# Threshold attention and two MoE layers: turned row maxima in `zt`'s spare columns, a start from two queues, decoding jobs further apart

## The chip, the cores and the metric

One core of a Trainium2 chip. The metric is the device time of one execution in microseconds; for the kernel before it is 1000.67 us, the median of 3 runs (996.61 to 1002.05).

## What is computed

Attention over 4 batches of 8 heads, 576 positions, head size 64, with a threshold under each row's maximum; then two feed-forward layers on the 2304 tokens.

```python
scores = scale * np.matmul(q, k.transpose(0, 1, 3, 2))
thresh = np.max(scores, axis=-1, keepdims=True) - tau
scores = np.where(scores >= thresh, scores, -1000000000.0)
attn = np.exp(scores - np.max(scores, axis=-1, keepdims=True))
attn = attn / (np.sum(attn, axis=-1, keepdims=True) + 1e-09)
x = np.matmul(attn, v)                      # then (tokens, heads * 64)
h = x @ w_in                                # 512 -> 2048
g = np.where(h >= 1, h, np.where(h <= -1, 0.0, (h + 1) ** 2 / 4))
y = g @ w_out
h2 = y @ w_in2                              # 512 -> 1024
solu = h2 * softmax(h2)
ln = (solu - mean(solu)) / np.sqrt(var(solu) + 1e-06) * g_ln
out = ln @ w_out2
```

## The kernel before

The program is in three stages: attention, the first feed-forward layer, the second. Matmuls take every operand as a high and a low part, so most products run as several. Only the attention stage and its start are touched by the diff.

Attention goes over 16 pairs of heads. A head's q and k (loaded side by side by `load_kq` into `nat`) are transposed together (`transpose_kq`, tile `tr`), split into a high half `q_st` on ScalarE and a low half `lo` on VectorE (`split_kq`), and copied by DMA into the stacked operands `k_both` (planes `k_st` and `k_on`), `q_st` and `q_m` (`stack_k`, `stack_q`). The scores are computed twice. First by rows: `scores` makes five tiles `sc` a head, `row_max` (VectorE) takes each row's maximum into `mcol`, and `row_shift` (two steps on ScalarE, three on GpSimd) makes of it the shift `mr`, 128 x 10. `shift_turn` transposes `mr` on TensorE (tile `tm`), `shift_store` copies it out on ScalarE (`mt`) and writes it by a DMA on ScalarE's queue into two more rows of `q_m`. Then by columns: `shifted` makes the transposed scores `zt` with the shift already subtracted; `expo` (ScalarE) takes the exponential `e`, `mask` (VectorE) sets to zero what lies under the threshold, `p_split` makes `phi` (ScalarE) and `plo` (GpSimd), and `values` multiplies them with v into `av`, three units later. `store_head` copies the sum out (`xs`).

A pair is 9 units. The order in which a unit's work is issued is a string in the table `ORDER`, a letter for each piece: E is `zt` and `e`, S a score, x a row maximum, M the mask, v and V values, P a transposition or a turn, A ScalarE's work on a shift or on v, T DMAs and other late work, F the split, J a step of a decoding job. The dictionaries `first_`, `late_`, `pe_` and so on hold what each unit does. The attention starts at unit `U0`; pair p's first `zt` is in unit 9p, and its scores run in the units `S_UNITS` before and after it.

`sc`, `zt`, `tr` and `tm` all take a tile of the PSUM pool `ps_r`, of 3 slots of two banks each. In a `zt` tile columns 288 to 511 of each bank are unused. `jobs` decodes and splits eight blocks of weights for the first feed-forward group meanwhile (VectorE, ScalarE and GpSimd), a new block every `JOB_EVERY` units.

## Time and profile before

| | |
|---|---|
| median of 3 runs | 1000.67 us |
| the profiled execution | 997.45 us |
| its span | 995.6 us |
| TensorE busy | 953.3 us (96%) |
| VectorE, ScalarE, GpSimd busy | 707.0, 499.3, 604.0 us |
| attention, 150 to 250 us: TensorE, VectorE, ScalarE, GpSimd busy | 94.70, 79.28, 70.10, 80.95 us |

A span is from the first to the last instruction of an execution; the time also holds what lies around it. The share of TensorE is a mean over stages: near the whole in the feed-forward stages, less in the attention, little in the first 20 us. In rows, PE is TensorE, PEld its weight loads, DVE VectorE, ACT ScalarE, POOL GpSimd, and SPq and ACTq the issuing of DMAs from SP and ScalarE. A row's L number is the line of the kernel.

### The profile page before, as it was taken

What the parts mean: (1) busy time and instruction counts of PE and PEld (TensorE: products, weight loads), DVE (VectorE), ACT (ScalarE), POOL (GpSimd) and SP (SyncE); (2) the same over time, 40 slices, a digit from 0 to 9 for tenths busy, and PEclk for the clock granted to TensorE, in tenths of its full rate; (3) what the DMA queues carried; (4) which work ended last, traced back from release to release, by engine and by line L of the source; (5) the groups of instructions that cost most, each with busy time, mean ns of one, the idle gap of its engine ahead of it and who ended that gap; (6) DMA issues with size and microseconds to landing.
All of it is one profiled execution on the core that took longest, in us unless ns stands there. A gap on an engine that the chain in (4) does not pass through costs nothing.

```text
span 995.6 us, 15113 instructions
## 1 busy us (share of the span) xinstructions
PE 953.3 (96%) x5232; PEld 840.2 (84%) x5232; DVE 707.0 (71%) x1128; ACT 499.3 (50%) x926; POOL 604.0 (61%) x573
## 2 busy tenths in 40 slices
PE   4999999999999999999999999999999999999998
PEld 3889888898898898889988998899889988888886
DVE  3678777778778765598858885887766576566661
ACT  3576776676676667444433333333334434434433
POOL 6477777887897788677535653555357804443422
PEclk9899999999999999999999999999999999999999
DMA  6555566566665421322221222122301214444443
GB/s 157 121 130 135 132 132 164 135 156 145 157 149 113 103 67 33 99 76 66 83 74 58 70 65 74 45 74 72 117 22 54 64 42 118 127 117 126 125 125 92
DMA packets 89885, 99.89 MB, mean 100 GB/s; under 512 B 50032, under 2 KB 62640, under 8 KB 89808
## 3 DMA queue, kind: packets, MB, share of 16 engines
q1 hardware_dynamic: 89424, 98.76, 38.7%
q8 instruction: 41, 0.67, 0.3%
q14 instruction: 36, 0.29, 0.1%
q10 hardware_dynamic: 384, 0.16, 0.1%
HBM read 55.13 MB, written 15.88 MB: 71 GB/s over the span
## 4 chain that ended last, share of the span: by engine, by line
PE 63%; DVE 14%; ACT 6%; POOL 6%; issue 6%; DMA 2%; SPq 2%; ACTq 1%; POOLq 0%; DVEq 0%
PE y L788 19%; PE h L750 19%; PE av L424 7%; PE zt L376 6%; PE sc L303 4%; DVE e L392 3%; POOL plo L401 2%; PE o L943 2%; PE h L832 2%; ACT e L387 2%; DVE so L860 2%; PE tr L260 2%; DVE so L887 2%; DVE st L848 1%; DVE so L872 1%
## 5 line engine op out<-in xcount | busy, mean ns | idle before, releaser
L401 POOL TENSOR_TENSOR plo<-e,phi 128x576 fp32r<-128x576 f32 x144 | 206.2, 1437 | 68.3 <-ACT phi L400 65.6
L771 POOL TENSOR_TENSOR gl<-cl,gh 128x512 fp32r<-128x512 f32 (+1 forms) x80 | 100.4, 1256 | 166.1 <-ACT gh L770 92.7
L788 PE MATMUL y<-gh,wg 128*128 128x512 f32 (+1 forms) x640 | 186.8, 373 | 0.0
L750 PE MATMUL h<-xh,wg 128*128 128x512 f32 (+1 forms) x640 | 184.1, 369 | 0.7 <-DVE e L392 0.7
L392 DVE SCALAR_TENSOR_TENSOR e<-zt,ntau,e 128x576 f32<-128x576 f32 x144 | 116.8, 812 | 78.6 <-ACT e L387 77.8
L387 ACT ACTIVATE e<-zt 128x576 f32<-128x576 f32 x144 | 93.7, 651 | 84.9 <-PE zt L376 69.2
L788 PEld LDWEIGHTS y<-gh,wg 128*128 128x128 f32 x640 | 118.8, 188 | 17.1
L750 PEld LDWEIGHTS h<-xh,wg 128*128 128x128 f32 x640 | 118.5, 188 | 17.4 <-DVE e L392 0.9
L788 PE MATMUL y<-gl,wg 128*128 128x512 f32 (+1 forms) x320 | 120.0, 375 | 0.5 <-POOL gl L771 0.4
L316 DVE TENSOR_REDUCE mcol<-sc 128x1 f32<-128x576 f32 x160 | 116.7, 748 | 3.2 <-PE sc L303 2.8
L750 PE MATMUL h<-xl,wg 128*128 128x512 f32 (+1 forms) x320 | 118.0, 369 | 0.0
L767 ACT ACTIVATE cl<-cl,half 128x512 f32<-128x512 f32 (+1 forms) x80 | 54.4, 680 | 98.3 <-DVE cl L766 98.0
L943 PE MATMUL o<-wg,ln 128*128 128x512 f32 x432 | 103.0, 394 | 0.4 <-ACT ln L906 0.4
L770 ACT CAST gh<-cl 128x512 fp32r<-128x512 f32 (+1 forms) x80 | 46.3, 579 | 111.6 <-DVE cl L769 105.0
L832 PE MATMUL h<-wg,y 128*128 128x512 f32 x432 | 101.1, 390 | 0.0
L943 PEld LDWEIGHTS o<-wg,ln 128*128 128x128 f32 x432 | 80.7, 188 | 19.9 <-ACT ln L906 1.8
L400 ACT CAST phi<-e 128x576 fp32r<-128x576 f32 x144 | 96.2, 668 | 0.9 <-DVE e L392 0.9
L832 PEld LDWEIGHTS h<-wg,y 128*128 128x128 f32 x432 | 81.0, 188 | 16.8
L907 POOL TENSOR_TENSOR ln<-land,ln 128x1024 fp32r<-128x1024 f32 x16 | 38.8, 2427 | 91.7 <-ACT ln L906 91.7
L766 DVE TENSOR_SCALAR cl<-h 128x512 f32<-128x512 f32 (+1 forms) x80 | 50.6, 632 | 56.2 <-PE h L750 52.3
L376 PE MATMUL zt<-q_st,k_both 128*128 128x288 f32 x320 | 75.6, 318 | 7.0 <-ACT mt L343 5.2
L303 PE MATMUL sc<-k_both,q_st 128*128 128x288 f32 x320 | 72.2, 308 | 5.3 <-DMA q_st<-lo 3.5
(107 smaller groups left out, 1871.9 us busy)
## 6 DMA issues: line engine op xcount, KB each, us to landing
raw<-in_moe_w_in_dram SPq DMA_DIRECT2D x24, 512.0 KB
raw<-in_moe_w_out_dram SPq DMA_DIRECT2D x24, 512.0 KB
k_both<-q_st SPq DMA_DIRECT2D x30, 288.0 KB
sq<-so SPq DMA_DIRECT2D x64, 128.0 KB
land<-sq SPq DMA_DIRECT2D x16, 512.0 KB
k_both<-lo SPq DMA_DIRECT2D x32, 144.0 KB
q_st<-lo SPq DMA_DIRECT2D x32, 144.0 KB
x<-xs SPq DMA_DIRECT2D x32, 144.0 KB
```

The source lines that it names most:

```text
L303: nc.tensor.matmul(ps[:, c, 0:HS], lhsT=st[j][i][r, n * P : n * P + P], rhs=kk[j][i][r, o + c * HS : o + (c + 1) * HS], start=(st is q_st) ...
L316: nc.vector.tensor_reduce(mc[:, n : n + 1], sc_ps.pop((h, n))[:, :, 0:HS], axis=AXES.XY, op=ALU.max, negate=True)
L376: nc.tensor.matmul(ps[:, c, 0:HS], lhsT=st, rhs=mv[:, c * HS : (c + 1) * HS], start=(m == 0), stop=(m == len(todo) - 1),)
L387: nc.scalar.activation(out=e, in_=st_ps[u][:, :, 0:HS], func=ACTF.Exp)
L392: nc.vector.scalar_tensor_tensor(out=e, in0=st_ps.pop(u)[:, :, 0:HS], scalar=ntau[:, 0:1], in1=e, op0=ALU.is_ge, op1=ALU.mult)
L400: nc.scalar.copy(hi, e)
L401: (nc.vector if u - NU in LO_DVE or u < NU - UNITS and u % UNITS in LO_UNITS else nc.gpsimd).tensor_tensor(lo, e, f32(hi), op=ALU.subtract)
L750: nc.tensor.matmul(ps, lhsT=a[:, kk, f], rhs=m[:, kk, :], start=(n == 0 and kk == 0), stop=(n == 2 and kk == KD - 1),)
L771: nc.gpsimd.tensor_tensor(gl, cl, f32(gh), op=ALU.subtract)
L788: nc.tensor.matmul(y_ps[c][d], lhsT=a[:, jj, ds_], rhs=m, start=(jj == 0 and n == 0), stop=(jj == JG - 1 and n == 2),)
L832: nc.tensor.matmul(ps[g], lhsT=a[:, kk, :], rhs=wg_t["in2", g][s][:, kk, :], start=(n < 2), stop=(n >= 6 * KD - 2),)
L943: nc.tensor.matmul(ps, lhsT=a[:, f, :], rhs=wg_t["out2", f // 4][m][:, f % 4, :], start=(n == 0), stop=(n == len(terms) - 1))
```

## The change

Three things are changed in the attention stage.

- **The turn.** `shift_turn` writes into columns 288 to 415 of the first bank of a unit's `zt` tile, behind `zt`'s matmuls, and `shift_store` follows that unit's `expo`. Before, it took a slot of its own at the end of a unit (`TURN_AT` 3); now it stands in the unit behind (`TURN_AT` 4): a pair's turns are in its unit 2 and in unit 7 of the pair before. Only the first head, whose turn comes before unit 0, still has a slot of its own.
- **The start.** `U0` is -10 instead of -18. The first pair's loads go alternately to SP's and ScalarE's queue. `split_first` replaces the first pair's `stack_k`: `k_st` and `k_on` are copied straight out of PSUM (ScalarE, VectorE), `q_m` on GpSimd. v of the first pair and half of the third pair's loads are issued from ScalarE. The second pair is transposed between the first pair's scores, its scores start in other units (`S_FIRST`), and `keep_warm` adds 18, 24 and four single transposes whose result nobody reads. The first weight block's load comes behind the stack copies, in unit -4.
- **Decoding.** Blocks start 16, 16, 16, 16, 17, 17, 12 and 10 units apart instead of 14.

```diff
-    U0 = -18
+    U0 = -10
     T_A, T_B = -16, -10
     S_UNITS = (-10, -9, -7, -7, -6, -5, -4, -3, -3, -2)
-    TURN_AT = 3
-    JOB_EVERY = 14
+    S_FIRST = ((-8, -7, -6, -5, -4, -3, -2, -1, -1, 0), (-8, -8, -7, -6, -6, -5, -4, -3, -3, -2))
+    WARM = (18, 24, 1)
+    TURN_AT = 4
+    JOB_EVERY = (16, 16, 16, 16, 17, 17, 12, 10)
...
-    FAST = 2
     V_POOL = 10
     LO_UNITS = ()
     NORM = (13, 6, 4)
     LO_DVE = ()
-    T_FIRST = (-17, -17)
-    T_SECOND = (-13, -2)
+    T_FIRST = (-10, -10)
+    T_SECOND = (-6, -1)
+    SPLIT_SECOND = (-3, 0)
...
+    def load_kq(p, other=nc.sync):
         t = early_p.tile([P, 2, NM + 1, 2, D], F32, tag="nat", name="nat", bufs=2)
         r0 = 2 * p * S
         two = q_rows[r0 : r0 + 2 * S, :].rearrange("(j s) d -> j s d", j=2)
-        for j in range(2):
-            nc.sync.dma_start(
-                t[:, j, 0:NM, 1, :], two[j, 0:M4, :].rearrange("(p t) d -> p t d", t=NM)
-            )
-        nc.sync.dma_start(t[0:64, :, NM, 1, :], two[:, M4:S, :].rearrange("j s d -> s j d"))
         k0 = k_rows[r0 : r0 + M4, :].rearrange("(p t) d -> p t d", t=NM)
         k1 = k_rows[r0 + M4 + P : r0 + 2 * S, :].rearrange("(p t) d -> p t d", t=NM)
+        rest = [
+            (t[0:64, j, NM * (1 - j), 0, :], k_rows[r0 + M4 + 64 * j : r0 + M4 + 64 * j + 64, :]) for j in range(2)
+        ]
+        main = [(t[:, j, 0:NM, 1, :], two[j, 0:M4, :].rearrange("(p t) d -> p t d", t=NM)) for j in range(2)]
+        nc.sync.dma_start(*main[0])
+        other.dma_start(t[0:64, :, NM, 1, :], two[:, M4:S, :].rearrange("j s d -> s j d"))
         nc.sync.dma_start(t[:, 0, 0:NM, 0, :], k0)
+        other.dma_start(*rest[0])
+        nc.sync.dma_start(*main[1])
+        other.dma_start(*rest[1])
         nc.sync.dma_start(t[64:P, 1, 0:NM, 0, :], k1[0:64])
-        nc.sync.dma_start(t[0:64, 1, 1 : NM + 1, 0, :], k1[64:P])
-        for j in range(2):
-            nc.sync.dma_start(t[0:64, j, NM * (1 - j), 0, :], k_rows[r0 + M4 + 64 * j : r0 + M4 + 64 * j + 64, :])
+        other.dma_start(t[0:64, 1, 1 : NM + 1, 0, :], k1[64:P])
...
     def stack_k(h):
         j, i = buf(h)
-        kh = f32(q_st[j][i][0:D, 0:S])
         o = slice(key_off(h), key_off(h) + S)
-        if h < FAST:
-            nc.scalar.copy(k_on[j][i][0:D, o], kh)
-            nc.scalar.copy(q_m[j][i][0:D, 0:S], f32(q_st[j][i][D:P, 0:S]))
-            nc.sync.dma_start(f32(k_st[j][i][0:D, o]), f32(k_on[j][i][0:D, o]))
-        else:
-            nc.sync.dma_start(f32(k_both[j][i][0:D, :, o]), kh.unsqueeze(1).to_broadcast([D, 2, S]))
+        kh = f32(q_st[j][i][0:D, 0:S]).unsqueeze(1).to_broadcast([D, 2, S])
+        nc.sync.dma_start(f32(k_both[j][i][0:D, :, o]), kh)
         nc.sync.dma_start(f32(k_st[j][i][D:P, o]), f32(tr_t[h][0:D, :]))
-        if h < FAST:
-            return
         nc.sync.dma_start(f32(q_m[j][i][0:D, 0:S]), f32(q_st[j][i][D:P, 0:S]))
 
     def stack_q(h):
         j, i = buf(h)
         nc.sync.dma_start(f32(q_st[j][i][0:D, 0:S]), f32(tr_t.pop(h)[D:P, :]))
+
+    def split_first():
+
+        srcs = [tr_t[h] for h in range(2)]
+        for h in range(2):
+            split_kq(h)
+            j, i = buf(h)
+            o = slice(key_off(h), key_off(h) + S)
+            nc.scalar.copy(k_st[j][i][0:D, o], srcs[h][0:D])
+            nc.vector.tensor_copy(k_on[j][i][0:D, o], srcs[h][0:D])
+            nc.sync.dma_start(f32(k_st[j][i][D:P, o]), f32(tr_t[h][0:D, :]))
+            stack_q(h)
+            nc.gpsimd.tensor_copy(q_m[j][i][0:D, 0:S], f32(q_st[j][i][D:P, 0:S]))
+
+    def keep_warm(n):
+
+        ps = ps_av.tile([P, 2, 512], F32, tag="av", name="av")
+        for _ in range(n):
+            nc.tensor.transpose(ps[:, 0, 0:P], ident, ident)
...
-    def shift_turn(h):
-        ps = ps_r.tile([P, 1024], F32, tag="r", name="tm")
-        nc.tensor.transpose(ps[0 : 2 * NTI, 0:P], f32(mr_t.pop(h)).rearrange("p l n -> p (l n)"), ident)
-        mr_t[h] = ps
+    def shift_turn(h, ps=None):
+
+        if ps is None:
+            ps = ps_r.tile([P, 2, 512], F32, tag="r", name="tm")
+        tm = ps[0 : 2 * NTI, 0, HS : HS + P]
+        nc.tensor.transpose(tm, f32(mr_t.pop(h)).rearrange("p l n -> p (l n)"), ident)
+        mr_t[h] = tm
 
     def shift_store(h):
         j, i = buf(h)
         mt = att_p.tile([2 * NTI, P], F32R, tag="mt", name="mt", bufs=2)
-        nc.scalar.copy(mt, mr_t.pop(h)[0 : 2 * NTI, 0:P])
+        nc.scalar.copy(mt, mr_t.pop(h))
         nc.scalar.dma_start(f32(q_m[j][i][R1:R3, :]), f32(mt))
...
+        for h in turn_in.get(u, ()):
+            shift_turn(h, ps)
         st_ps[u] = ps
...
-            self.todo, self.depth = [(t, every, True) for t in todo], depth
+            self.todo, self.depth = [(t, n, True) for t, n in zip(todo, every)], depth
...
+    load_kq(0, nc.scalar)
     nc.scalar.activation(out=warm, in_=one, func=ACTF.Exp)
-    load_kq(0)
...
-            at(first_, t + 1, split_kq, h)
-            at(late_, t + (STACK[0] if h >= FAST else 1), stack_k, h)
-            at(late_, t + (STACK[1] if h >= FAST else 1), stack_q, h)
+            if p:
+                t = t + 1 if p > 1 else SPLIT_SECOND[j]
+                at(first_, t, split_kq, h)
+                at(late_, t + (STACK[0] - 1 if p > 1 else 0), stack_k, h)
+                at(late_, t + (STACK[1] - 1 if p > 1 else 1), stack_q, h)
             at(last_, UNITS * p + (4, 8)[j] + LAGV, store_head, h)
-        if p > 1:
+        if p > 2:
             at(late_, UNITS * p + T_A - 5, load_kq, p)
         if p:
-            at(late_, UNITS * p - 16, load_v, p)
-        at(act_, UNITS * p + V_AT, split_v, p)
+            at(late_, UNITS * p - 16 if p > 1 else -5, load_v, p)
+        if p:
+            at(act_, UNITS * p + V_AT, split_v, p)
+    at(late_, -2, split_v, 0)
...
+        s_units = S_FIRST[p] if p < 2 else S_UNITS
+        for n, d in enumerate(s_units):
             at(s_at, UNITS * p + d, None, 2 * p + n // NTI, n % NTI)
         for j in range(2):
-            t = UNITS * p + S_UNITS[NTI * j + NTI - 1]
+            t = UNITS * p + s_units[NTI * j + NTI - 1]
             at(act_, t + 1, row_shift, 2 * p + j)
-            at(pe_, t + TURN_AT, shift_turn, 2 * p + j)
-            at(act_, t + TURN_AT, shift_store, 2 * p + j)
+            t += TURN_AT if p else 2
+            if t < 0:
+                at(pe_, t, shift_turn, 2 * p + j)
+                at(act_, t, shift_store, 2 * p + j)
+            else:
+                turn_in.setdefault(t, []).append(2 * p + j)
...
                 expo(u)
+                for h in turn_in.get(u, ()):
+                    shift_store(h)
...
-    jobs.step()
     load_kq(1)
-    load_v(0)
-    setup_fill(True)
-    at(late_, T_FIRST[1] + 1, setup_fill, False)
+    setup_fill(0, nc.gpsimd)
+    setup_fill_v()
+    keep_warm(WARM[0])
+    at(pe_, U0 + 1, keep_warm, WARM[1])
+    at(first_, U0 + 1, split_first)
+    at(late_, U0 + 1, load_v, 0, nc.scalar)
+    at(late_, U0 + 1, load_kq, 2, nc.scalar)
+    at(late_, U0 + 1, setup_ones)
+    at(late_, U0 + 1, setup_fill, 1, nc.gpsimd)
+    at(late_, 0, setup_fill, 2, nc.gpsimd)
+    at(late_, -4, jobs.step)
+    for u in (-8, -7, -5, -4):
+        at(late_, u, keep_warm, WARM[2])
```

The rows of the kernels' order show three places. First SP at the start: what is issued up to the first pair's stack copies (128x4x64, 64x2x64 and so on are the loads of q and k; names with 98, 101, 103 and 106 are the first pair's operands). Before, from the second pair's last load:

```order
L227 DMA nat<-in_k_dram 64x64 x2
L237 DMA v_nat_113<-in_v_dram 128x2x256
L243 DMA v_nat_113<-in_v_dram 64x64 x2
L281 DMA k_both_98<-k_both_98 64x576
L284 DMA k_both_98<-lo 64x576
L291 DMA q_st_103<-lo 64x576
```

And of the change:

```order
L231 DMA nat<-in_k_dram 64x64
L232 DMA nat<-in_k_dram 64x4x64
L233 DMA nat<-in_k_dram 64x4x64
L301 DMA k_both_98<-lo 64x576
L290 DMA q_st_103<-lo 64x576
```

No v and no weight block stand ahead of the stack copies now, and the copy of the high half is gone.

Second, TensorE at the first head's turn of a pair, where unit 6 gives way to unit 7. Before:

```order
L424 MATMUL av<-plo,v_hi_116 128x288
L337 MATMUL tm<-ident,mr 10x128 [waits DVE_49,Pool_49]
L376 MATMUL zt<-q_st_107,k_both_102 128x288 [waits Activation_49]
L376 MATMUL zt<-q_st_107,k_both_102 128x288
```

And of the change:

```order
L398 MATMUL zt<-q_st_107,k_both_102 128x288 [waits DVE_49]
L398 MATMUL zt<-q_st_107,k_both_102 128x288
L398 MATMUL zt<-q_m_112,k_both_102 128x288 x2
L358 MATMUL zt<-ident,mr 10x128 [waits Pool_49]
L448 MATMUL av<-phi,v_hi_116 128x288 [waits Activation_49]
```

The turn stands behind `zt` and waits for GpSimd alone; `zt` no longer waits for ScalarE.

Third, ScalarE at the same turn. Before:

```order
L343 CAST mt<-tm 10x128 [waits DMAHW5_49,PE_49]
L344 DMA q_m_111<-mt 2x5x128 [waits DMAHW6_49,Activation_49]
L387 ACTIVATE e<-zt 128x576 [waits PE_49,Pool_49]
L436 COPY xs<-av 128x576 [waits PE_49]
L400 CAST phi<-e 128x576 [waits DVE_49]
```

And of the change:

```order
L411 ACTIVATE e<-zt 128x576 [waits PE_49]
L364 CAST mt<-zt 10x128 [waits DMAHW3_49]
L365 DMA q_m_111<-mt 2x5x128 [waits DMAHW4_49,Activation_49]
L460 COPY xs<-av 128x576 [waits DMAHW5_49,PE_49]
L424 CAST phi<-e 128x576 [waits DVE_49]
```

The exponential moved ahead of the copy and its DMA. On VectorE the mask behind such an exponential has new waits:

```order
L416 SCALAR_TENSOR_TENSOR e<-zt,ntau,e 128x576 [waits Activation_49] x2
L416 SCALAR_TENSOR_TENSOR e<-zt,ntau,e 128x576 [waits PE_49,Activation_49,Pool_49]
L334 TENSOR_REDUCE mcol<-sc 128x1 [waits PE_49] x2
```

Its row names TensorE beside ScalarE, where the masks of the two units before name ScalarE alone.

## Rows read from the trace of the kernel before

**Rows 1.** Busy time of each engine in stretches of the program (us, busy, instruction counts, granted clock, DMA share, GB/s)

```profile
150.00:250.00 100.00, 94.70 (x676) 88.78 (x674) 79.28 (x111) 70.10 (x133) 80.95 (x81) 1.00 0.64 152
...
500.00:600.00 100.00, 100.00 (x480) 87.65 (x480) 77.22 (x116) 35.83 (x59) 51.28 (x40) 1.00 0.21 66
```

**Rows 2.** Waits of TensorE, 60 to 385 us (waiter, waited for: us, times, longest)

```profile
PE tr L260 <- DVE e L392: 7.5, 11, 0.8
PE zt L376 <- ACT mt L343: 4.8, 14, 0.3
...
PE tm L337 <- POOL mr L330: 1.4, 5, 0.4
```

**Rows 3.** The chain in order of time, 150 to 200 us (start, us, what)

```profile
163.56 0.64 PE tr L260 x5
...
168.85 0.11 PE tm L337
168.96 0.55 PE zt L376 x4
...
182.14 0.29 PE tm L337
...
182.76 0.79 PE zt L376 x4
...
194.81 0.86 PE tr L260 x5
```

**Rows 4.** Timeline, unit 2 of a pair (start, us, engine, line, out<-in, idle before)

```profile
191.79 0.43 PE L376 MATMUL zt<-q_m,k_both 67*128 67x288 f32 x2
...
192.25 0.25 ACT L343 CAST mt<-tm 10x128 fp32r<-10x128 f32 x1
...
192.53 0.62 ACTq L344 DMA_DIRECT2D q_m<-mt  x1
...
193.25 0.65 ACT L387 ACTIVATE e<-zt 128x576 f32<-128x576 f32 x1 [0.75 <-PE av L424]
...
193.94 0.82 DVE L392 SCALAR_TENSOR_TENSOR e<-zt,ntau,e 128x576 f32<-128x576 f32 x1 [1.29 <-ACT e L387]
```

**Rows 5.** Timeline, 0 to 24 us: loads, splits, first stack copy, first score

```profile
1.19 1.33 SPq L217 DMA_DIRECT2D nat<-in_q_dram  x2
...
6.38 1.09 PE L260 MATMUL tr<-ident,nat 128*128 128x128 f32 x4 [6.38 <-POOL q_m L188]
...
8.15 0.74 ACT L268 ACTIVATE q_st<-tr,scale 128x576 fp32r<-128x576 f32 x1 [5.93 <-PE tr L260]
...
8.93 0.82 DVE L269 SCALAR_TENSOR_TENSOR lo<-tr,scale,q_st 128x576 fp32r<-128x576 f32 x1 [4.73 <-ACT q_st L268]
...
10.20 0.66 ACT L279 CAST k_both<-q_st 64x576 fp32r<-64x576 f32 x1
...
13.02 1.11 SPq L243 DMA_DIRECT2D v_nat<-in_v_dram  x2
...
14.26 0.52 SPq L281 DMA_DIRECT2D k_both<-k_both  x1
...
18.24 0.82 PE L303 MATMUL sc<-k_both,q_st 128*128 128x288 f32 x2 [3.46 <-DMA q_st<-lo]
```

**Rows 6.** The chain in order of time, 0 to 90 us

```profile
15.46 2.64 DMA q_st<-lo
```

**Rows 7.** Timeline, 24 to 60 us: `zt` of unit 0 and of unit 4

```profile
27.89 0.42 PE L376 MATMUL zt<-q_st,k_both 128*128 128x288 f32 x2
...
39.26 0.43 PE L376 MATMUL zt<-q_st,k_both 128*128 128x288 f32 x2
```

**Rows 8.** Busy time and granted clock in stretches of 2 us

```profile
34.00:36.00 2.00, 1.77 (x7) 1.10 (x7) 1.73 (x3) 0.21 (x2) 1.41 (x1) 0.50 0.86 219
```

**Rows 9.** Timeline, GpSimd near the turn at 182 us and after it

```profile
181.89 0.20 POOL L330 TENSOR_TENSOR mr<-sh,mr 128x5 fp32r<-128x5 f32 x1
...
184.80 2.81 POOL L401 TENSOR_TENSOR plo<-e,phi 128x576 fp32r<-128x576 f32 x2
```

More of the change, by code (lines that the diff above doesn't have):

```diff
@@ L173, in setup, with setup_fill, setup_fill_v, setup_ones @@
         nc.vector.tensor_tensor(ntau, tau_sb, ntau, op=ALU.min)
-    def setup_fill(first):
-        for i in range(max(NBUF)):
-            for j in range(2):
-                if i >= NBUF[j] or (i == 0) != first:
-                    continue
-                pad = slice(S, SP) if j == 0 else slice(0, 64)
-                nc.gpsimd.memset(f32(k_st[j][i][:, pad]), 0.0)
-                nc.gpsimd.memset(f32(k_on[j][i][:, pad]), 0.0)
-                nc.gpsimd.memset(f32(k_on[j][i][D:R3, 64 * j : 64 * j + S]), 1.0)
-                nc.gpsimd.memset(f32(k_on[j][i][D:R1, 64 * j : 64 * j + S]), 0.0)
-                nc.gpsimd.memset(f32(q_st[j][i][:, S:SP]), 0.0)
-                nc.gpsimd.memset(f32(q_m[j][i][0:D, S:SP]), 0.0)
-                nc.gpsimd.memset(f32(q_m[j][i][D:R3, :]), 0.0)
-        for t in v_nat if first else ():
+    def setup_fill(i, eng):
+        for j in range(2):
+            if i < NBUF[j]:
+                pad = slice(S, SP) if j == 0 else slice(0, 64)
+                eng.memset(f32(k_st[j][i][:, pad]), 0.0)
+                eng.memset(f32(k_on[j][i][:, pad]), 0.0)
+                eng.memset(f32(k_on[j][i][D:R3, 64 * j : 64 * j + S]), 1.0)
+                eng.memset(f32(k_on[j][i][D:R1, 64 * j : 64 * j + S]), 0.0)
+                eng.memset(f32(q_st[j][i][:, S:SP]), 0.0)
+                eng.memset(f32(q_m[j][i][0:D, S:SP]), 0.0)
+                eng.memset(f32(q_m[j][i][D:R3, :]), 0.0)
+    def setup_fill_v():
+        for t in v_nat:
             nc.gpsimd.memset(t[64:P, 8, :], 0.0)
             nc.gpsimd.memset(t[0:64, 9, :], 0.0)
-        for t in () if first else v_hi:
+    def setup_ones():
+        for t in v_hi:
             nc.gpsimd.memset(f32(t[:, 0:8, D:P]), 1.0)
@@ L236, in load_v @@
         for js, src in main_rows(v_rows, p):
[L237 removed]
+            eng.dma_start(
                 t[:, 4 * js.start : 4 * js.stop, :].rearrange("p (j t) d -> p j (t d)", t=NM),
@@ L359 @@
     st_ps = {}
+    turn_in = {}
     e_t = {}
@@ L990 @@
     begin = {(0, 0, 2): 0, (1, 0, LAGO): 1, (2, 0, LAGO): 2, (3, 0, LAGO): 3, (3, 1, 0): 4, (3, 2, 0): 5}
-    jobs = Jobs([], 0, 3)
+    jobs = Jobs([], (), 3)
     fine[0], WAIT[0], AFTER_ADD[0] = False, 2, 1
```

8 lines of the change are left out of this document (2 added, 6 removed).

## Prediction

> **What bounds the kernel now.** I read the busy time by stage first. In the MoE stages TensorE is busy 100 of 100 us [rows 1]; nothing in the diff touches what runs there, so those stages stay as they are. In the attention stage, before them, TensorE is busy 94.7 of 100 us, with VectorE at 79 and GpSimd at 81: TensorE is the bound there and its idle time is the only thing to win. TensorE's first score is at 18.24 us [rows 5]; before it there are a few transposes and waits for data. So there are two places to look at: the start, and the regular stalls.
>
> For the regular stalls I read who TensorE waited for between 60 and 385 us, about 14 pairs of heads. Nearly all is two items: the transposes `tr` waiting for the mask (7.5 us in 11 waits), and `zt` waiting for the ScalarE copy `mt` (4.8 us in 14), with `tm` waiting for GpSimd's `mr` behind them (1.4 us in 5) [rows 2]. The chain in order of time shows that each costs more than its idle time, since the pipelined matmuls drain and refill. Where a turn is stalled, `tm` plus the next `zt` run from 182.14 to 182.76 + 0.79 = 183.55, that is 1.41 us; where it isn't, 0.11 + 0.55 = 0.66 us. So 0.75 us a time. A stalled `tr` takes 0.86 us against 0.64 [rows 3], on top of 7.5 / 11 = 0.68 us of idle: 0.90 us a time. Together 14 x 0.75 + 1.4 + 11 x 0.90 = 21.8 us are lost to these two places.
>
> **The turn inside `zt`.** Before, `tm` takes a PSUM slot of its own and the next `zt` takes that same slot, so it waits until `mt` has been read out. Now `tm` is written into unused columns of `zt`'s own tile, behind `zt`. It is still one transpose; it needs no slot, and `zt` (0.55 us) runs while `mr` is finished, so the wait for `mr`, at most 0.4 us, is covered too. I take the whole first stall as removed: 14 x 0.75 + 1.4 = 11.9 us.
>
> The second stall goes by way of ScalarE. In unit 2 of a pair `mt` and its DMA issue (0.62 us from 192.53) stand ahead of the exponential `e`, which starts at 193.25 though its `zt` was done at 191.79 + 0.43 = 192.22; the mask follows at 193.94 and `tr`, which takes the mask's slot, starts at 194.81 [rows 4]. Now `e` goes first, which is 0.25 + 0.62 = 0.87 us earlier. The mask doesn't gain all of that: in the new order the mask behind such an `e` waits for TensorE and ScalarE anew, and I read this as a wait for `mt` (0.25 us plus a hand-over of some 0.04), because it reads the same PSUM tile. So the mask comes 0.55 to 0.6 us earlier, and of a wait of 0.68 about 0.1 to 0.2 us is left, with `tm`'s 0.11 us now on the path. I keep 0.7 of the 0.90 us, 11 x 0.7 = 7.7 us.
>
> That is a rule that speaks against this change: "PSUM — Partial Sum Buffer" of the Trainium skill, section Terms, says that TensorE, ScalarE and VectorE must not be in one bank and quadrant at a time, reads against reads included. By it every turn orders `zt`, `tm`, `e`, `mt` and mask one behind the other. No run here shows what an overlap does; the order agrees, in that the exponential now waits for `tm`. Without the rule the mask would gain 0.87 us and the second term would be 9.9 us instead of 7.7.
>
> **What is late next.** Both terms, 19.6 us, hold if the others keep up. ScalarE still does the same work; `xs` and `phi` behind the turn start no earlier than now, while TensorE comes 0.75 to 1.1 us earlier, so a later exponential and mask in the next unit will be reached by `zt` at 0.2 to 0.3 us of wait. Two such places a pair, 28 in all, half of them hit at 0.3 us give back 4.2 us. I take 15 us for the steady part. The ends are 5 us, if most of the stall turns into waits for masks and GpSimd, and 21.8 us.
>
> **The start.** Before, the first stack copy (L281) leaves SP at 14.26, although ScalarE wrote its source from 10.20 on for 0.66 us [rows 5]: it stood behind 20 issues (two pairs' q and k of 8 each, one weight block, 3 for v) that took SP from 1.19 to 14.14, 0.65 us each. Now 12 stand ahead of it, 4 of the first pair (the other 4 on ScalarE's queue) and 8 of the second: 1.19 + 12 x 0.65 = 9.0. The data is ready at about the same time: the first pair's loads are issued by about 3.8 instead of 6.5, the 18 warm-up transposes take 18 x 0.27 = 4.9 us from the finished identity on and end near 6.2 at the pace of the first row of `tr` (1.09 us for 4), then five transposes (1.4), the high half (0.74) and the low half (0.82) [rows 5] end at about 9.2. The second copy leaves near 9.9 and lands 2.64 us later, as `q_st` did [rows 6]: scores start at about 12.5 to 13 instead of 18.24, 5.5 us earlier.
>
> From the first score to the first `zt` it was 27.89 - 18.24 = 9.65 us [rows 5, 7]. This stays: five row maxima, shift, turn, store and its landing. ScalarE now has 7 DMA issues (3 for v, 4 for the third pair) of 0.62 us, 4.3 us, ahead of the third head's split. VectorE's low half of that head stands ahead of the second head's maxima, which so wait some 0.9 us. GpSimd's fills move behind the copies `q_m`; they end before the shift needs GpSimd. The `v` split and `setup_fill` of the third buffer come before unit 0's `plo` and the second turn: at most 1 us.
>
> From the first `zt` to that of unit 4 it took 39.26 - 27.89 = 11.4 us [rows 7], with TensorE at the lower of its two clock levels, 0.50 (1.2 GHz), around 34 to 36 us [rows 8]. VectorE has 4 masks and 2 low halves of 0.82 us [rows 4, 5] and 6 maxima, which I put at about the same, in this stretch: 12 x 0.82 = 9.8 us with no wait. So 0 to 1.6 us can be won. Start in all: 5.5 - 0.9 + 1.6 = 6.2 us, and I take 6.5, since the wake-up transposes may hold the clock up; the ends are 3 (one microsecond lost at each of the three steps and no gain after the first `zt`) and 9 (SP free and data ready 2.5 us sooner). The single wake-up transposes between scores take 0.27 us each at that pace and lie in TensorE's idle time.
>
> **Decoding spread.** The eight weight blocks are the same; their starts go from 14 to 16 or 17 units apart. That takes about a tenth of the decode work out of each pair and puts it in pairs that have none. VectorE and GpSimd aren't the bound; the last block starts near unit 108 of 144 and is done before the MoE stage. Nothing, in either direction, is what I take; it is covered by TensorE's 94.7%.
>
> **Sum.** 15 + 6.5 = 21.5 us off the profiled execution's 997.45 us (span 995.6 us) gives 976.0. That execution lies 3.2 us below the median of 1000.67 of the three runs; I put the forecast between them, **977 us**. About 0.5% (5 us) is what a measurement of this kernel can tell from no change.
>
> **Rivals.**
> 1. *The stall only changes its name.* GpSimd is busy 80.95 of 100 us [rows 1], and `mr` came at 181.89 + 0.20 [rows 9], after TensorE was free for its turn. If GpSimd and the mask chain set the period, the steady part gives 5 us and the start 6.5: 986 us. For it: VectorE and GpSimd at about 80%, three PSUM slots. Against: outside these stalls TensorE waits for almost nothing [rows 2]. Chance 0.2.
> 2. *All of it goes*, 21.8 + 9 = 31 us: 966 to 969 us. Chance 0.15.
> 3. *Slower.* `e` now waits for `tm`, and `tm` for `mr`, which stands among pieces of `plo` on GpSimd, 1.41 us each (2.81 for two, [rows 9]). If one more piece gets ahead of `mr`, it is late by 1.41 us; of this 0.75 us only repeats the stall removed and 0.55 us is covered by `zt` in the first kind of turn. In the second kind TensorE, the exponential and the mask all stop. It decides from an `mr` 1.3 us later than now, at both turns; two more pieces, 2.82 us, then cost 28 x 1.5 = 42 us against 21.5 won: 1018 us. Against: `mr` was late in 5 waits of 28 only [rows 2]. Chance 0.03.
> 4. *The start gets worse or gains nothing* since ScalarE sits in its DMA issues and the slots fill with the third head, while the steady part gives 10: 988 us; with 5 or less it can't be told from no change. Chance 0.1.
>
> **Numbers.** The forecast's own case has 0.52, with 970 to 983 us. The range 964 to 990 takes in rivals 1 and 2 and part of 4. Faster by over 0.5%: 0.52 + 0.2 + 0.15 and a third of rival 4, 0.9. Within 0.5%: 0.07. Slower: 0.03.
>
> **What would show it.** In the changed profile the wait of `zt` for `mt` is gone from TensorE's waits and that of `tr` for the mask is under 3 us; the period of a pair falls by about 1.1 us; the first score stands at 12 to 13.5 us, the first `zt` near 22, and unit 4's near 33. It is wrong if new waits of TensorE for masks, maxima or `mr` add to over 10 us, or if the first score comes after 15 us.

## The result, and the profile after

The changed kernel takes **989.79 us** (median of 4 runs, 988.53 to 990.8) against 1000.72 us of the kernel before on the same chip: ratio 0.991 [0.988, 0.994]. That is faster by 11 us where 24 were forecast. It lies at the upper edge of the range (990) and where rival 4 put it (988: the start gains nothing, the steady part gives 10). The profiled execution took 990.58 us, span 988.8 us.

Busy time by stage, the columns as in [rows 1]; the last three stretches are the start:

```profile
150.00:250.00 100.00, 96.50 (x684) 89.89 (x684) 78.46 (x108) 69.11 (x135) 82.38 (x82) 1.00 0.66 153
500.00:600.00 100.00, 100.00 (x481) 87.65 (x480) 77.24 (x116) 35.79 (x59) 51.55 (x39) 1.00 0.21 66
...
14.00:20.00 6.00, 6.00 (x27) 5.49 (x26) 3.51 (x5) 0.74 (x1) 3.12 (x10) 0.52 0.73 164
20.00:27.00 7.00, 6.09 (x33) 4.57 (x31) 5.30 (x9) 2.94 (x7) 3.06 (x8) 0.93 0.68 175
27.00:38.00 11.00, 10.18 (x40) 9.30 (x41) 6.54 (x9) 5.47 (x11) 6.09 (x10) 0.54 0.62 137
```

The MoE stage is untouched. In the attention TensorE is busy 96.5 us of 100 instead of 94.7. In the start it is nearly full, but at a granted clock of 0.52 and 0.54 in two of the three stretches: it works at 1.2 GHz, not 2.4, in most of 14 to 20 and 27 to 38 us.

TensorE's waits from 60 to 385 us, to set against [rows 2]:

```profile
PE zt L398 <- DVE lo L275: 4.3, 9, 0.6
PE sc L321 <- DVE e L416: 2.3, 3, 1.7
PE av L448 <- ACT xs L460: 1.6, 3, 0.8
PE sc L321 <- DMA v_nat<-in_v_dram: 1.5, 1, 1.5
```

`zt` waiting for `mt` and `tr` waiting for the mask are gone from these waits. `zt` of unit 4 now takes the PSUM slot of `tr` and waits until VectorE's `lo` has read it (4.3 us in 9 waits; before, 0.7 us in one). New is a score that waited 1.66 us and 1.52 us in two pairs.

The turn in unit 2 of a pair, beside [rows 4]:

```profile
191.86 0.43 PE L398 MATMUL zt<-q_m,k_both 67*128 67x288 f32 x2
...
192.12 0.27 PE L358 MATMUL zt<-ident,mr 128*10 128x128 f32 x1
...
192.44 0.66 ACT L411 ACTIVATE e<-zt 128x576 f32<-128x576 f32 x1
192.99 0.24 ACT L364 CAST mt<-zt 10x128 fp32r<-10x128 f32 x1
...
193.31 0.82 DVE L416 SCALAR_TENSOR_TENSOR e<-zt,ntau,e 128x576 f32<-128x576 f32 x1 [0.47 <-ACT mt L364]
...
194.18 0.86 PE L266 MATMUL tr<-ident,nat 128*128 128x128 f32 x5
```

The mask stands 1.45 us behind the last `zt` matmul instead of 2.15, and it does wait for `mt` behind `e`, as the prediction read it.

The start, in the columns of [rows 5] and [rows 7]:

```profile
13.04 0.50 PE L321 MATMUL sc<-k_both,q_st 128*128 128x288 f32 x2 [2.38 <-DMA q_st<-lo]
...
15.06 0.68 PE L321 MATMUL sc<-k_both,q_m 65*128 65x288 f32 x2
...
16.93 0.74 ACT L274 ACTIVATE q_st<-tr,scale 128x576 fp32r<-128x576 f32 x1 [5.64 <-DMA nat<-in_k_dram]
...
24.27 0.43 PE L398 MATMUL zt<-q_st,k_both 128*128 128x288 f32 x2
...
27.82 0.80 PE L321 MATMUL sc<-k_both,q_st 128*128 128x288 f32 x2 [1.01 <-DVE e L416]
28.41 0.68 PE L321 MATMUL sc<-k_both,q_m 65*128 65x288 f32 x2
...
38.08 0.43 PE L398 MATMUL zt<-q_st,k_both 128*128 128x288 f32 x2
38.35 0.43 PE L398 MATMUL zt<-q_m,k_both 67*128 67x288 f32 x2
```

A pair of 288-column matmuls shows 0.43 us at the upper clock level (the next starts 0.27 us later) and 0.68 at the lower (0.48 later): each slow pair costs 0.21 us more. The first score is 5.2 us earlier than before, `zt` of unit 0 3.6 us, `zt` of unit 4 only 1.2 us. Behind the score that waited at 27.82 us every pair is slow until 38 us.

### The profile page after: what moved, and what is told of

It reads as the page before. It is cut to its first block, busy times and chain, and to the rows that moved or that the text cites. A ratio compares the mean times of both kernels' runs of the same rounds, so it can differ in the third digit from the quotient of the medians.

```text
span 988.8 us, 15140 instructions
## 1 busy us (share of the span) xinstructions
PE 965.4 (98%) x5278; PEld 850.6 (86%) x5278; DVE 713.5 (72%) x1130; ACT 494.1 (50%) x924; POOL 605.0 (61%) x575
## 4 chain that ended last, share of the span: by engine, by line
PE 73%; DVE 7%; ACT 5%; POOL 4%; DMA 4%; issue 3%; SPq 2%; ACTq 0%; DVEq 0%; POOLq 0%
PE y L824 20%; PE h L786 19%; PE o L979 10%; PE h L868 10%; PE av L448 5%; PE zt L398 4%; PE sc L321 3%; DVE e L416 3%; POOL plo L425 2%; DVE mcol L334 2%; ACT e L411 2%; ACT phi L424 1%; DMA nat<-in_k_dram 1%; PE tr L266 1%; DVE lo L275 1%
```

## The experiments

One table for all. T is the first turn of the second pair; "slow" counts the slow pairs (0.60 us or more) among the 66 to 68 pairs of 288-column matmuls from the first score to T; the last column is T to the last turn of the attention, 14.5 pairs, called the steady part below. Times are medians, ratios are to the kernel before on the same chip; the positions are of one profiled execution each. How far such a row can differ by itself shows in five kernels whose start is the same up to unit 2 (the change, e16, e4, e5, e8): first score 13.04 to 14.62 us, `zt` of unit 0 23.62 to 26.46, T 45.61 to 47.23, 17 to 32 slow pairs.

| kernel | us | ratio [95%] | first score | `zt` unit 0 | T | slow | steady |
|---|---|---|---|---|---|---|---|
| before | 996.0 to 1000.7 | 1 | 18.24 | 27.89 | 46.24 | 18 | 325.6 |
| the change | 989.79 | 0.991 [0.988, 0.994] | 13.04 | 24.27 | 45.61 | 26 | 320.4 |
| e16 the change again | 990.77 | 0.992 [0.989, 0.994] | 13.05 | 23.62 | 46.97 | 32 | 316.5 |
| e1 turn only | 986.83 | 0.989 [0.986, 0.992] | 18.29 | 28.18 | 45.01 | 9 | 315.6 |
| e2 start only | 998.47 | 1.001 [1.000, 1.003] | 14.16 | 25.50 | 45.72 | 21 | 327.2 |
| e8 even decoding | 987.69 | 0.990 [0.987, 0.992] | 14.62 | 25.74 | 46.65 | 17 | 316.7 |
| e12 mask first | 1013.73 | 1.017 [1.014, 1.019] | 14.50 | 26.66 | 49.33 | 29 | 339.8 |
| e4 V later | 985.51 | 0.988 [0.985, 0.991] | 14.24 | 25.41 | 46.24 | 20 | 320.9 |
| e5 copy earlier | 986.46 | 0.989 [0.986, 0.991] | 14.30 | 26.46 | 47.23 | 23 | 314.5 |
| e9 e1 and copy earlier | 985.12 | 0.989 [0.986, 0.991] | 18.29 | 27.87 | 44.69 | 7 | 314.5 |
| e3 warm at unit 1 | 986.62 | 0.989 [0.985, 0.992] | 13.12 | 26.89 | 46.76 | 28 | 316.2 |
| e6 no warming | 990.43 | 0.993 [0.991, 0.996] | 13.06 | 26.20 | 48.28 | 44 | 316.7 |
| e7 more warming | 989.04 | 0.992 [0.989, 0.994] | 13.00 | 24.16 | 47.24 | 30 | 316.9 |
| e10 e5, loads on SyncE | 987.41 | 0.990 [0.988, 0.992] | 12.82 | 21.84 | 49.42 | 19 | 313.9 |
| e11 e10, warmed | 988.30 | 0.992 [0.989, 0.994] | 12.80 | 21.30 | 47.88 | 21 | 316.3 |
| e13 e5, load later | 984.43 | 0.986 [0.984, 0.989] | 12.98 | 24.46 | 45.25 | 21 | 314.1 |
| e14 e13, holes filled | 984.90 | 0.986 [0.983, 0.988] | 14.62 | 24.66 | 46.10 | 15 | 314.8 |
| e15 e9 with warming | 987.80 | 0.988 [0.986, 0.991] | 18.31 | 28.84 | 48.85 | 32 | 315.4 |
| e17 e14, all holes | **981.12** | **0.983 [0.980, 0.986]** | 14.45 | 22.95 | 42.77 | **0** | 314.5 |

### Which part of the change does it: e1, e2, e8

e1 is the kernel before with the turn of pairs 1 to 15 in `zt`:

```
-            at(pe_, t + TURN_AT, shift_turn, 2 * p + j)
-            at(act_, t + TURN_AT, shift_store, 2 * p + j)
+            if p:
+                turn_in.setdefault(t + 4, []).append(2 * p + j)
+            else:
+                at(pe_, t + TURN_AT, shift_turn, 2 * p + j)
+                at(act_, t + TURN_AT, shift_store, 2 * p + j)
...
```

> The kernel before with the turn moved into the free columns of zt (pairs 1 to 15, four units behind the last score) and nothing else: its start, its loads and its decoding stay. Theory A (the turn's removed waits come back elsewhere): the attention from the first turn to the last falls by about 5 us as in the comparison of the two traces (318.3 to 313.0), so the ratio to before is 0.993 to 0.997; the waits tr<-mask (7.5 us) and zt<-mt (4.8 us) are gone from the profile and zt<-DVE lo (about 4 us) stands in their place. Theory B (the turn is worth the forecast 15 us, and the new start or the new decoding takes it back): ratio 0.985 or lower, and the steady stretch shorter by 12 us or more.

e2 is the change with that one part undone:

```
-            t += TURN_AT if p else 2
-            if t < 0:
+            t += 3 if p else 2
+            if p or t < 0:
```

> The changed kernel with the turn of every pair but the first put back into a slot of its own, three units behind the last score, as before; start and decoding stay changed. Theory A (the start's gain is eaten by half clock): first score at 13 us as in the change, zt of unit 4 near 38 us against 39.3 before, ratio to before 0.997 to 1.0. Theory B (the start is worth the forecast 6.5 us and the loss is all in the steady part): zt of unit 4 at 33 to 36 us, ratio 0.992 to 0.995.

e8 sets `JOB_EVERY = (14,) * 8` in the change:

> The changed kernel with the decoding of the first weights at the old even pace (a new block every 14 steps) instead of the spread one. Theory A (the prediction's term of 0: no engine that TensorE waits for is late for the decoding): same time as the change within 1 us, steady part between 316 and 321 us. Theory B (the spread is what keeps VectorE and GpSimd free where the low halves are due): zt<-DVE lo above the 4.3 us of the change, time 2 us or more longer.

The turn alone gives the whole gain, ratio 0.989, that is 11.4 us (8.5 to 14.2). That lies between what theory A (0.993 to 0.997) and theory B (0.985) of that run expected; the steady part is 10.0 us shorter, nearer to B's 12 than to A's 5. Its waits from 60 to 385 us:

```profile
PE zt L380 <- DVE lo L269: 3.6, 7, 0.7
PE av L430 <- ACT xs L442: 1.7, 3, 0.8
PE av L430 <- POOL plo L407: 0.9, 3, 0.4
```

The start alone gives nothing that could be told, +1.4 us (-0.3 to +3.1): theory A of e2, though its first score is at 14.16 us. In its profile T is 0.5 us earlier than before and the steady part 1.6 us longer. The decoding's pace makes no difference that could be told: with the even pace the time is 987.69 and the steady part 316.7, within what e16 shows. The term of 0 stands.

### The score that waited in two pairs: e4, e5, e9

In the change the copy of q's low half stands on SyncE's queue behind the store of the finished head, which cannot leave before ScalarE's `xs`:

```profile
79.06 0.24 SPq L462 DMA_DIRECT2D sums<-xs  x1
79.35 0.46 SPq L463 DMA_DIRECT2D x<-xs  x1
79.91 0.55 SPq L290 DMA_DIRECT2D q_st<-lo  x1
...
84.25 0.50 PE L321 MATMUL sc<-k_both,q_st 128*128 128x288 f32 x2 [1.66 <-DVE e L416]
```

My first guess was the V load beside it (e4):

```
-            at(late_, UNITS * p - 16 if p > 1 else -5, load_v, p)
+            at(late_, UNITS * p - 13 if p > 1 else -5, load_v, p)
```

> The changed kernel with the load of a later pair's V (256 KB and two rests) issued three units later, so that it no longer lies beside the stacking copies of the second head (issued at 79.9 and 80.6 us in the change). Theory A (the first score of the second head waits for those copies at 84.25 and 154.04 us because the V load shares the queue): both waits (1.7 and 1.5 us) are gone, with the half clock behind the first of them (86 to 90 us), and the time falls by 3 to 5 us against the change. Theory B (the score waits for a slot, that is for the mask before it, whatever the queue does): the waits stay and the time is the same within 1 us.

The guess fell: both waits stayed, 1.34 us at 84.58 and 2.33 us at 154.26, the second now put down to a stacking copy, and the steady part was 320.9. So in e5 the copy itself was moved ahead, `STACK = (1, 2)` for `(1, 3)`. In the changed kernel this acts from the third pair on, not from the third head as the expectation says:

> The changed kernel with the copy of q's low half (q_st<-lo) issued one unit earlier for every head from the third on, so that on SyncE's queue it stands before the store of a finished head, which waits for ScalarE's xs, and not behind it. In the change it is issued 3.4 us before the first score of the second head in most pairs, and that score waits 1.7 and 1.5 us in two pairs (lags of 4.3 and 4.9 us), each time with a slower pair (24.6 and 23.7 us instead of 22.2). Theory A (that score waits for this copy, whose landing varies from run to run): no pair has that wait, every pair takes under 23 us, steady part near 316 us instead of 320.4, time 985 or less with a narrower spread of the runs than the change (984 to 991). Theory B (what lands late is another transfer, or the mask): waits and spread stay, same median as the change within 1 us.

In e9 the same on top of e1, where it acts from the second pair on:

> The kernel before with two edits alone: the turn in the free columns of zt (as in the run with the turn only) and the copy of q's low half issued one unit earlier. Start, loads and decoding are those of before. Theory A (the turn is the whole gain and the earlier copy takes away the pairs that were slow now and then): no score of a second head waits over 0.5 us after 45 us, steady part 314 to 316 us, ratio to before 0.985 to 0.989 and the spread of the runs under 5 us. Theory B (the earlier copy does nothing here, or costs by colliding with the copies of k): ratio 0.989 or more, spread as wide as with the turn alone (984.4 to 990.9).

In e5 the copy leaves at 78.03 us, ahead of `sums<-xs` at 80.68. No pair has such a wait, the steady part is 314.5, and the runs lie between 984.8 and 987.0 (e16: 987.6 to 992.0). Of the eight kernels with the early copy six have a steady part under 315 us (e15 has 315.4, and e11 316.3, where one score still waited 1.31 us for the copy, at 196 us); with the turn in `zt` and the late copy none is under 315.6. That is theory A by the profiles. The time doesn't tell e5 from the change (0.989 [0.986, 0.991] and 0.991 [0.988, 0.994]). In medians e9 and e1 can't be told apart either, and e9's runs still spread over 6.5 us (982.9 to 989.4).

### The order of the two reads: e12

```
                 expo(u)
-                for h in turn_in.get(u, ()):
-                    shift_store(h)
...
                 mask(u)
+                for h in turn_in.get(u, ()):
+                    shift_store(h)
```

> The changed kernel with ScalarE's copy of the turned maxima (mt) placed behind VectorE's mask of the same tile instead of ahead of it. In the change that mask stands still for mt (0.48 us at 77.7 us). Theory A (this holds VectorE, and so the low half lo in the unit after, for which zt of unit 4 waits): the row zt<-DVE lo falls from 4.3 us to 1.5 us or less and the time by 2 to 4 us. Theory B (lo is late for its own reasons, the mask's wait lies in VectorE's slack): zt<-DVE lo stays at 4 us and the time is the same within 1 us.

Both theories missed: 24 us slower than the change. The timeline at a turn:

```profile
192.92 0.82 DVE L416 SCALAR_TENSOR_TENSOR e<-zt,ntau,e 128x576 f32<-128x576 f32 x1 [0.37 <-ACT e L411]
...
193.77 0.25 ACT L364 CAST mt<-zt 10x128 fp32r<-10x128 f32 x1 [0.88 <-DVE e L416]
...
194.79 0.64 ACT L460 COPY xs<-av 128x576 f32<-128x576 f32 x1 [0.77 <-ACT mt L364]
...
195.49 0.53 PE L448 MATMUL av<-phi,v_hi 128*128 128x288 f32 x2 [0.61 <-ACT xs L460]
```

and ScalarE's waits from 60 to 385 us:

```profile
ACT mt L364 <- DVE e L416: 26.0, 28, 1.7
```

`mt` now waits for the mask, 0.93 us at each turn, and ScalarE stands with it; `xs`, for which the next head's `av` waits, comes late (8.7 us of TensorE's waits in 14), and `lo` waits longer as well (8.0 us in 13). In neither order do the two reads of the tile overlap: the second reader waits for the first. That is what "PSUM — Partial Sum Buffer" of the Trainium skill, section Terms, asks for (two engines not in one bank and quadrant, reads included). Both orders keep to it, so no run here shows what an overlap would do; they do show which of the two engines can afford to wait: VectorE.

### Where the start's gain goes: e3, e6, e7

e3 adds `keep_warm(6)` behind `zt` of unit 1, e6 sets `WARM = (0, 0, 0)`, e7 `WARM = (18, 42, 1)`:

> The changed kernel with six more throw-away transposes of the identity behind zt of unit 1, where TensorE now stands still for 1.0 us (a score at 27.82 waits for the mask) and the granted clock is 0.50 from there to 38 us. Theory A (that idle stretch brings the clock down): the granted clock stays at 1.0 from 24 to 38 us, zt of unit 4 comes 4 to 5 us earlier (33 to 34 us instead of 38.1), and the time falls by 4 to 5 us against the change (ratio to before near 0.987). Theory B (the clock falls for what went before, or for a reason that filling this hole doesn't touch): granted clock 0.50 in 28 to 38 us as in the change, same time within 1 us.

> The changed kernel without the throw-away transposes at the start (those behind the loads, behind the first turn and between the first scores). Theory A (work without holes is what keeps the clock up): the clock falls as early as in the change or earlier, unit 4 at 38 us or later, time the same or up to 3 us longer. Theory B (the throw-away work itself, 42 transposes before the first score at 13.04 us, brings the clock down right after it, since the kernel before has none of it and keeps 1.00 up to 32 us): granted clock 1.00 from 13 to 24 us, zt of unit 0 at 22 us instead of 24.3, time 3 to 5 us shorter.

> The changed kernel with 18 more throw-away transposes behind the first turn (42 instead of 24), which fill the hole from 10.7 to 13.0 us in front of the first score. Theory A (the hole brings the clock down at 15 us): granted clock 1.00 from 13 to 24 us, zt of unit 0 near 22 us instead of 24.3, time 2 to 4 us shorter. Theory B (the clock falls for the work done, not for the hole): granted clock 0.50 from 14 us or earlier, same time within 1 us or longer.

e7 filled the hole ahead of the first score, and the clock held to 20 us, then fell where the first head's own turn waited 1.26 us for `mr`: 30 slow pairs, all behind that. In e3 every pair was slow from the first score on, behind 2.75 us of waiting, to 32.8 us; the hole that it filled came too late to matter, so it doesn't tell its theories apart. e6 has most, 44 slow pairs, from the first score, behind a wait of 5.04 us, to 41 us, though TensorE hardly stands still after it; theory B of that run is out. In time none of the three can be told from the change by the intervals. In e6 the granted-clock column shows 1.00 over all of the slow stretch:

```profile
24.00:40.00 16.00, 15.90 (x61) 13.83 (x61) 9.74 (x14) 7.66 (x14) 8.53 (x14) 1.00 0.51 110
```
```profile
38.08 0.68 PE L323 MATMUL sc<-k_both,q_st 128*128 128x288 f32 x2
38.56 0.68 PE L323 MATMUL sc<-k_both,q_m 65*128 65x288 f32 x2
```

so at the start the level has to be read from the matmuls themselves; in [rows 5] too the first score of the kernel before shows 0.82 us, a slow one. "TensorE: Matmul & The Clock Gate" of the Trainium skill, section Seeing it yourself, warns that the recorded clock events aren't reliable; this row agrees.

### Holes, or what the loads hold up: e10, e11, e13 to e17

e10 is e5 with the seven loads that ScalarE issued put on SyncE; e11 adds transposes in the holes (42; 8 ahead of the first turn; 3 and 6 behind `zt` of units 0 and 1):

```
-    at(late_, U0 + 1, load_v, 0, nc.scalar)
-    at(late_, U0 + 1, load_kq, 2, nc.scalar)
+    at(late_, U0 + 1, load_v, 0)
+    at(late_, U0 + 1, load_kq, 2)
```

> The changed kernel with the earlier copy of q's low half, and with the loads of the first V and of the third pair's q and k, of which the change issues seven on ScalarE's queue behind the first split, all put on SyncE's. Theory A (these issues hold ScalarE, whose split of the third head stands at 16.9 us behind them, and with it the masks, maxima and turns of units 0 and 1): that split starts at 15 us or earlier, zt of unit 0 at 23 us or earlier, first matmul of the stage behind the attention 1 to 3 us earlier than in the run with the earlier copy alone (375.96). Theory B (the split waits for its transposed tile and TensorE's clock, not for ScalarE): same time within 1 us of that run (986.5), or later by what SyncE's queue then holds back.

> The same as the run before, with throw-away transposes in every hole of the start that TensorE shows: 42 instead of 24 behind the first turn, 8 ahead of the first head's own turn (a hole of 1.4 us), 3 behind zt of unit 0 and 6 behind zt of unit 1. Theory A (holes are what brings the clock down): granted clock 1.00 from 13 to 38 us, zt of unit 4 at 33 to 34 us, first matmul of the stage behind the attention near 371 us, 5 us earlier than with the earlier copy alone. Theory B (a start that works this densely from 4 us on is put to half clock anyway): 15 us or more at granted 0.50 between 13 and 40 us, same time as the run before within 1.5 us.

In e10 `zt` of unit 0 came at 21.84 us, where the prediction had it, with no slow pair before it. But a score then waited 6.74 us at 31 us for a copy behind the loads on SyncE's queue (SP in the rows), and behind it every pair was slow until 42.6 us. In e11 that wait was 3.19 us, with 21 slow pairs behind it and behind an earlier wait of 1.21 us. The time came as theory B has it in both. e13 issues only the third pair's load later, `at(late_, -2, load_kq, 2)`:

> The changed kernel with the earlier copy of q's low half, and with the load of the third pair's q and k issued seven units later and wholly on SyncE, behind the stacking copies of the third head, so that it holds neither ScalarE (the change) nor those copies (the run with all of them on SyncE, where a score waited 6.7 us at 31 us). Theory A (the start's gain is lost to what these issues hold up): zt of unit 0 at 22 us or earlier, no wait over 1 us behind it, second pair's first turn at 43 us or earlier (45.6 in the change), time 983 or less. Theory B (TensorE is put to half clock in this start whatever is held): 10 us or more at half speed between the first score and that turn, the turn at 45 us or later, time 985 to 988.

e14 fills the holes on top, with 8 transposes inside `zt` of unit 0 where it waits for `q_m<-mt`:

> The same with throw-away transposes in the holes that the earlier runs showed: 42 behind the first turn, 8 ahead of the first head's own turn, 8 inside zt of unit 0 where it waits for the turned maxima's copy, 6 behind zt of unit 1. Theory A (each hole of about a microsecond is what brings the clock down, and there is none left): under 4 us at half speed between the first score and the second pair's first turn, that turn at 40 to 42 us, time 981 or less. Theory B (the fall comes without a hole as well): 10 us or more at half speed, the turn at 45 us or later, time 985 to 989.

e13 no longer has e10's wait of 6.74 us, and still 21 slow pairs: theory B, by its count and by T. But two holes were left, and each of its two groups of slow pairs lies behind one of them (to 20.7 and 37.9 us):

```profile
12.98 0.50 PE L321 MATMUL sc<-k_both,q_st 128*128 128x288 f32 x2 [2.45 <-DMA q_st<-lo]
...
30.86 0.38 PE L358 MATMUL zt<-ident,mr 128*10 128x128 f32 x1 [1.23 <-POOL mr L348]
```

In e14 the slow pairs are 15, in two groups, each behind a hole that was left: 2.36 us ahead of the first score, and 1.07 us at the turn of unit 2:

```profile
28.78 0.42 PE L321 MATMUL sc<-k_both,q_st 128*128 128x288 f32 x2
...
31.71 0.27 PE L358 MATMUL zt<-ident,mr 128*10 128x128 f32 x1 [1.07 <-POOL mr L348]
...
33.72 0.85 PE L398 MATMUL zt<-q_st,k_both 128*128 128x288 f32 x2
```

e15 puts the throw-away transposes into the old start, e16 is the change again:

> The kernel with the old start, the turn in zt and the earlier copy, with 18 and 24 throw-away transposes added at its beginning as the change has them. Theory A (early throw-away work is what makes the clock fall later on): 10 us or more at half speed between the first score and the second pair's first turn (3.3 without it), that turn at 46.5 us or later instead of 44.7, time 987 or more. Theory B (it warms the engine and no more): the half speed of the first scores (18.3 to 22 us) is gone, the turn at 43.5 us or earlier, time 983 to 984.5.

> The changed kernel itself, beside the others on the same chip. Theory A (the old start with the turn and the earlier copy, 985.1 us, is the faster of the two, by the 3 to 4 us that the new start loses to half clock): 988 to 990 us. Theory B (the difference is one of chips): 985 to 986.5 us.

e15's profile has 32 slow pairs instead of 7 and T 4.2 us later: theory A of that run. Its time does not differ from e9's by the intervals, and the kernel before, with the same start and no throw-away work, has 18. So waking TensorE early and then letting it stand (4.17 us ahead of the first score here) saved no slow pairs. e16 came at 990.77 us, near theory A. The cleaner pair is e5 and e9, which differ in the start and the decoding alone: both are at 0.989 [0.986, 0.991], so the new start gains nothing there either. e17 fills both holes of e14:

```
-    WARM = (18, 42, 1)
+    WARM = (18, 54, 1)
...
+        if u == 2:
+            keep_warm(9)
         for h in turn_in.get(u, ()):
             shift_turn(h, ps)
```

> The run before last but two (late load, holes filled) with its two remaining holes filled as well: 54 instead of 42 transposes behind the first turn (its first score waited 2.4 us and the clock fell at 15.3 us), and 9 ahead of the turn in zt of unit 2 (1.07 us of waiting for mr, and the clock fell at 32.1 us). Theory A (a hole of a microsecond or more is what the clock falls behind): under 4 us at half speed between the first score and the second pair's first turn (12.2 us there), that turn at 41 to 43 us instead of 46.1, time 980 to 982. Theory B (the clock falls without such a hole as well): 8 us or more at half speed, the turn at 44.5 us or later, time 983 to 986.

The start of e17 and three of its rows:

```profile
14.00:20.00 6.00, 5.41 (x37) 4.88 (x38) 4.17 (x7) 1.25 (x3) 2.37 (x8) 1.00 0.68 186
20.00:27.00 7.00, 6.92 (x54) 6.29 (x53) 5.20 (x8) 3.15 (x6) 3.61 (x10) 1.00 0.68 150
27.00:38.00 11.00, 9.67 (x69) 8.55 (x68) 7.32 (x10) 6.00 (x13) 5.65 (x10) 1.00 0.71 163
```
```profile
22.95 0.43 PE L398 MATMUL zt<-q_st,k_both 128*128 128x288 f32 x2
...
30.03 0.28 PE L358 MATMUL zt<-ident,mr 128*10 128x128 f32 x1
...
35.26 0.43 PE L398 MATMUL zt<-q_st,k_both 128*128 128x288 f32 x2
```

There is no slow pair, the longest wait left is 0.99 us ahead of the first score, T is at 42.77 us, and the six runs lie between 980.4 and 982.8 us. Their mean granted clock is 0.998 to 1.000, where six runs of e16 have 0.989 to 0.994 (a mean that can miss a slow start, as e6 shows; the profiled run's matmuls don't). With 0.983 [0.980, 0.986] against 0.992 [0.989, 0.994] of e16 it beats the change, and with it the kernel before. The numbers of theory A came: 0 slow pairs, where the other 14 profiles with this start have 15 to 44. But the time tells e17 neither from e13 nor from e14 by the intervals, so what the filling is worth in time isn't measured alone; the level and T show it.

Nor is "a hole of a microsecond or more" what the clock falls behind. The kernel before went slow at 32 us with no wait of TensorE over 0.43 us from 20 us on:

```profile
31.39 0.53 PE L376 MATMUL zt<-q_st,k_both 128*128 128x288 f32 x2 [0.36 <-DVE e L392]
...
32.12 0.67 PE L303 MATMUL sc<-k_both,q_st 128*128 128x288 f32 x2
```

So did e15, at 32.34 us behind a wait of 0.36 us. e1 and e9 have the same 0.36 us at 31.7 and 31.4 us and stay fast. Whether it is the place of the throw-away work or its amount (85 transposes up to T in e17, 66 in e14) that kept the level up was not separated.

## Why the prediction was wrong

**The turn: right in mechanism, too large.** Both waits went as said, `e` before `mt`, `mt` before the mask. Of the 15 us, 11.4 (8.5 to 14.2) came, 10.0 in the profiled steady part. The mis-sized step is the price of a stall. I put 8.1 us for draining and refilling on top of the idle time (21.8 instead of 7.5 + 4.8 + 1.4 = 13.7) and gave back 4.2. In e1 TensorE's waits from 40 to 400 us shrink from 19.7 to 7.7 us, by 12.0, and the steady part by 10.0: the idle time was the price, the mark-up was not there to win. What I gave back to late masks came back in a place I had not named, `zt` of unit 4 behind `lo` (4.3 us), since the slots rotate differently. Rival 1 was right by that much. A pair takes 0.69 us less in e1 (10.0 / 14.5) and 0.36 in the change's profile, not 1.1. In the change's own profile the late copy took another 3.2 us of waiting.

**The start: the step that failed.** It is the path from the first score to `zt` of unit 4. Ahead of it the account held: the first score came at 13.04 for 12.5 to 13, against [rows 5]. That was partly luck. In all 15 kernels with this start SyncE issues the second stack copy at 10.27 to 10.37 us, and the first score, which waits for it, stands at 12.8 to 13.1 us in 8 profiles and at 14.2 to 14.6 in 7: the 2.64 us of [rows 6] is one landing of several.

Then "this stays", of the 9.65 us from there to `zt` of unit 0, was wrong: 11.23 us. And from there to unit 4 I priced VectorE's work alone and let 11.4 us fall towards 9.8: it took 13.81. The term was -6.5 us with ends of 3 and 9 gained; measured alone it is +1.4 (-0.3 to +3.1), outside both. Two things stand in its place.

*Work that moved.* `S_FIRST` puts eight more score matmuls between `zt` of unit 0 and of unit 4 (46 matmuls of 288 columns instead of 38), and the second pair's first five transposes now stand behind the first score (15 up to T instead of 10). In e17, which has no slow pair, unit 0 to unit 4 still takes 35.26 - 22.95 = 12.31 us, with 23 throw-away transposes among them. In e1, with the old order and without a slow pair there either, it takes 9.33:

```profile
28.18 0.43 PE L380 MATMUL zt<-q_st,k_both 128*128 128x288 f32 x2
...
37.51 0.42 PE L380 MATMUL zt<-q_st,k_both 128*128 128x288 f32 x2
```

That is earlier than the change's 38.08, though e1's first score is 5.2 us later. No run gives this work a price of its own.

*The clock.* I had the row of the lower clock [rows 8] and read it as something a few wake-up transposes would mend. They do not: 17 to 32 slow pairs in the five kernels with this start, 18 before. An earlier start moves the work to where TensorE waits (for the stacking copy, `mr`, a mask, `mt`'s copy), and behind such waits it ran at half speed in all of these profiles but e17's. At 0.21 us a pair, the change's 26 cost an estimated 5.5 us and the 18 before 3.8: the difference of 1.7 us is less than the 4.6 us that were lost between the first score (5.2 us earlier than before) and T (0.6 us earlier).

So the clock is a part of the loss. At full speed (e17) T is 3.5 us earlier than before and 1.9 us earlier than in e9, which has the old start: still not 6.5.

Rival 4 had the time nearly right, with 10 from the steady part, which gave 5.2 in the change's profile and 9.1 in e16's. Of its reason, ScalarE's DMA issues, the runs show only a part (`zt` of unit 0 at 21.84 without them in e10, with the clock as another difference). e13, which takes four of the seven off, is not told from e5 by its interval.

**Rival 3** did not come: from 60 to 385 us no wait of TensorE for `mr` is left in the change, and ScalarE's exponential has two (1.2 and 1.0 us). e12 shows that a turn that holds ScalarE has a price of that order, 24 us.

**The sum** added two independent terms. Within the intervals they do add: 11.4 - 1.4 = 10.0, and the change gave 11, and 8 in e16. The turn's term was too large; the start's had a wrong path.

## What to carry to other kernels

Price a stall at its idle time; count a drain and refill on top only where a run has shown it. Before counting an earlier start as gain, count the work that moves behind its first matmul, and look at what TensorE does from there to its steady pace: if it has holes, read the clock level from the matmuls and try to fill the holes with throw-away work up to the moment the data comes, as e17 did. Where one engine issues its DMAs in program order, as SyncE does here, put a copy that someone waits for ahead of a store that waits for someone else.
